# Attention and two feed-forward layers on one core: the first layer's rounding moved from VectorE to ScalarE, a third tile for decoded weights, and a new order of issue

## The chip, the cores and the metric

The kernel runs on one core of a Trainium2 chip, in one launch. The metric is the device time of that core in microseconds, the median of three runs. The engines are named as the profile names them: PE (TensorE, matrix multiply) with PEld (its weight loads), DVE (VectorE), ACT (ScalarE), POOL (GpSimd) and SP (SyncE, which here only issues DMAs). Each engine takes its own instructions strictly in the order in which they were written, so an instruction that waits holds up all that stand behind it on that engine.

## The reference

Three stages, one behind the other, in float32:

```python
# 1: attention, q, k, v of (4, 8, 576, 64): 32 heads
scores = scale * q @ k.T
thresh = max(scores, axis=-1) - tau
scores = where(scores >= thresh, scores, -1e9)
attn = exp(scores - max(scores)); attn = attn / (sum(attn) + 1e-9)
x = (attn @ v) as (2304, 512)
# 2: first feed-forward layer, w_in (512, 2048), w_out (2048, 512)
h = x @ w_in
x = (h * cos(h)) @ w_out
# 3: second feed-forward layer, its own weights
r = maximum(x @ w_in, 0)
out = (s * r * r + b) @ w_out
```

## The kernel before

**Attention.** The 32 heads are worked as 16 pairs of two heads, a pair as 9 tiles of 128 queries against 576 keys. One tile's chain is: PE forms the scores `s` (L318, L325) into one of two PSUM buffers; DVE reduces them to the row minimum `mn` (L332; keys are negated, so it stands for the maximum); POOL adds tau to it (`thr`, L336); ACT takes the exponential `e` (L340); DVE compares, multiplies and sums in one instruction (`p`, L346), which gives the score buffer back. PE turns finished tiles (`pt`, L281, and the rest of the tiles as `ptr`, L378), ACT stores them (L296, L300), and PE multiplies them with the values (`av`, L430), for the pair before, between the score tiles of the running pair. DVE's reciprocal of the row sums (`r<-sm`, L399) is issued once per pair.

**Weights.** They lie in DRAM as 64-bit words, 32 half blocks per layer: for each of 16 slices `f` of the hidden dimension, part 0 (input weights) and part 1 (output weights). `decode` (L179) makes two float tiles, `wh` and `wl`, from one half block: a DMA into a raw tile `wr` (two of them, L534), the magnitude on ACT (L538), a clamp on POOL (L542), three integer instructions on DVE, called shift, sign and fill here (L545, L550, L555), the high part `wh` (on POOL for the first 15 half blocks, L564, later on ACT, L568), and the low part `wl` on POOL (L189). Between the magnitude and `wl` the words lie in a tile `wt`, of which there are two. The first 15 half blocks of layer 1 (`EARLY`) have room in memory while attention runs; the other 17 get theirs when attention has ended. A half block's name in the rows is `wt_f_part`.

**Feed-forward layers.** Each layer runs over five blocks of tokens (four of 512, one of 256) and in each over the 16 slices, 72 steps of 512 columns per layer. One step has 12 hidden matmuls (`h`, L657, into one of four PSUM banks), the stages of the activation, and 12 output matmuls (`acc`, L758 in the first layer, L760 in the second). Products are formed three times, from high and low parts, so every operand is split in two. At a block's start its tokens are split into `x` tiles: ACT writes the high part (L631), DVE subtracts (L634, shown as L189) for each of 4 column groups. The stages of a first-layer step (L692 to L737) are: the rounding to integers `s0` on DVE, from the bank (L694, which the profile shows as helper line L687), the remainder `s1` on DVE (L697), a clamp on POOL (L700), the sine on ACT with the bias tile `hpi` (L705, helper line L226), the product with `h` on DVE (L708), which frees the bank, the high part `gh` on ACT, and the low part `gl` on POOL (L189). Stages of a step are called by these names below.

**The order.** Nothing is issued as it is written in the source. `Order` (L28) holds every piece of work with its engine, a length in nanoseconds that is written by hand (`add(engine, length, rank, ...)`), a rank and what it must wait for. `run` (L80) then plays the engines forward: each engine takes, of the first `WINDOW` pieces by rank, the first one that can begin within `SLACK` ns of the earliest, and the resulting order is the one that is issued. Ranks come from the tables `PAIR` and `PLACE` (L119 to L126): `early` and `early_step` set the rank, in pairs, of the 15 early half blocks; `first`, `second` and their steps that of the later ones. A tile whose buffers are all in use can't be drawn, so the sizes in `ring` (L219) shape the order as well.

Of the kernel before, what the change touches and what calls it, by code (L numbers as in the profile page):

```python
# [10 lines left out]
F32 = mybir.dt.float32  # L11
# [6 lines left out]
P = 128  # L18
# [9 lines left out]
class Order:  # L28
# [3 lines left out]

    SLACK = 262
    LAG = 90
    WINDOW = 48

# [77 lines left out]
EARLY = 15  # L116

WEIGH = (3, 4)
PAIR = 16840  # L119

PLACE = {
    "scores": -6086, "stat": -3181, "exp": -7313, "mask": 1993, "turn": 1108, "turned": 3152, "rest": 443,
    "rested": -1757, "sums": 1929, "weigh0": -252, "weigh1": 4687, "weigh_step": 1086, "finish": -4708,
    "normalise": 40063, "keys": -30127, "early": 3.337, "early_step": 1.142, "first": 3.121, "second": 1.354,
    "second_step": 0.963, "first_step": 0.523, "xin": -10749, "active": 5021, "output": 5748,
}  # L126
STEP = 5450

# [2 lines left out]
def attention_moe_moe2_kernel(  # L131
# [37 lines left out]
    nc.scalar.dma_start(out=tau_t, in_=tau)  # L169
    hpi = cpool.tile([P, 1], F32, name="hpi")  # L170
    nc.vector.memset(hpi, math.pi / 2)

    warm = cpool.tile([P, 1], F32, name="warm")
    nc.scalar.activation(warm, hpi, AF.Exp)
# [23 lines left out]

    for half in halves[:EARLY]:
        open_w(half)  # L200
    wtp = ctx.enter_context(tc.tile_pool(name="wtp", bufs=2))
    mg = ctx.enter_context(tc.tile_pool(name="mg", bufs=2))


# [13 lines left out]

    for name, size in (  # L219
        ("s", 2), ("pt", 4), ("q", 2), ("k", 1), ("ks", 2), ("v", 2), ("e", 2), ("p", 12), ("PT", 2),  # L220
        ("rb", 1), ("xs", 1), ("wr", 2), ("wt", 2), ("r", 2), ("gh", 2), ("gl", 2), ("mn", 6), ("thr", 6),
    ):
        ring(name, size)

# [8 lines left out]
    def pair(n):  # L233
# [70 lines left out]
        for i in range(9):  # L304
# [37 lines left out]
            def mask(i=i):  # L342
                if "sm" not in T:
# [4 lines left out]
                    accum_out=T["sm"][:, i : i + 1],  # L348
                )

            s_ = add("PE", 600 if i == mixed else 500, at + PLACE["scores"], scores, after=[lq, ks] if i == 0 else [], take=[ts],
                     give=[tk["q"], tk["ks"]] if i == 8 else [], tail=250)
            scored.append(s_)
            m_ = add("DVE", 755, at + PLACE["stat"], stat, after=[s_], take=[tm])
            t_ = add("POOL", 190, at + PLACE["stat"], limit, after=[m_], take=[th])
# [3 lines left out]
            if i in (1, 3, 4, 6, 8):  # L359
                tiles = [i] if i == mixed else [i - 1, i]  # L360
                tt = [ticket("pt"), ticket("pt")]
                r_ = add("PE", 280 * len(tiles), at + PLACE["turn"], lambda t=tiles: turn(t), after=[masks[j] for j in tiles],
                         take=[*tt, *([tk["PT"]] if i == 1 else [])], tail=170)
                for g in (1, 0):
                    c_ = add("ACT", 170 + 215 * len(tiles), at + PLACE["turned"], lambda g=g, t=tiles: store_turned(g, t),
                             after=[r_], give=[tt[g]])
                    transposed.append(c_)
# [152 lines left out]
    def decode(half, rank, opened):  # L520
# [53 lines left out]
        o = add("SP", 60, rank - 6000, load, take=[tr], tail=4000)  # L574
        o = add("ACT", 675, rank, magnitude, after=[o], take=[tt])
        o = add("POOL", 620 if early else 720, rank, clamp, after=[o])
        o = add("DVE", 430 if early else 600, rank, shift, after=[o])
        o = add("DVE", 690 if early else 1030, rank, sign, after=[o])
        o = add("DVE", 690 if early else 1150, rank, fill, after=[o], give=[tr])
        o = add("POOL" if early else "ACT", 630, rank, high, after=[o, opened], take=[tw])  # L580
        o = add("POOL", 1270 if early else 1370, rank, low, after=[o], give=[tt])
# [34 lines left out]
    def blocks_of(layer, blk):  # L616
# [25 lines left out]
        def step(fs):  # L642
# [43 lines left out]
            def mult_add(o, x, s1, s2_):  # L686
                nc.vector.tensor_scalar(out=o, in0=x, scalar1=s1, scalar2=s2_, op0=ALU.mult, op1=ALU.add)  # L687

            e = w / 0.96
            if layer == 0:  # L690

                def s0():  # L692
                    tiles()
                    mult_add(B["r"].bitcast(I32), B["h"], 1.0 / TWO_PI, 0.25)  # L694

                def s1():
                    nc.vector.scalar_tensor_tensor(B["r"], B["r"].bitcast(I32), -TWO_PI, B["h"], ALU.mult, ALU.add)  # L697

                def s2_():
                    nc.gpsimd.tensor_scalar(  # L700
                        out=B["r"], in0=B["r"], scalar1=RMAX, scalar2=RMIN, op0=ALU.min, op1=ALU.max
                    )

                def s3():
                    act(B["r"], B["r"], AF.Sin, bias=hpi)  # L705

                def s4():
                    nc.vector.tensor_tensor(B["r"], B["h"], B["r"], ALU.mult)  # L708

                def s5():  # L710
                    tiles_g()
                    act(B["gh"], B["r"], AF.Copy)

                stages = [
                    ("DVE", 150 + e, s0, [rt], []), ("DVE", 150 + e, s1, [], []), ("POOL", 790, s2_, [], []),
                    ("ACT", 720, s3, [], []), ("DVE", 150 + e, s4, [], [ht]), ("ACT", 630, s5, [ght], []),
                ]
            else:
                def s0():
                    tiles()  # L720
                    act(B["r"], B["h"], AF.Relu)

                def s1():
                    act(B["r"], B["r"], AF.Square)

                def s2_():
                    mult_add(B["r"], B["r"], s_t, b_t)

                def s3():
                    tiles_g()  # L730
                    nc.vector.tensor_copy(B["gh"], B["r"])  # L731

                stages = [
                    ("ACT", 600, s0, [rt], [ht]), ("ACT", 630, s1, [], []), ("DVE", 550, s2_, [], []),
                    ("DVE", 430, s3, [ght], []),
                ]
# [147 lines left out]
```

## Time and profile before

| | us |
|---|---|
| median of 3 runs (1146.82 to 1151.14) | 1147.77 |
| the profiled execution | 1150.11 |
| its span, first to last instruction | 1148.3 |
| PE busy | 1075.1 (94%) |
| DVE busy | 657.6 (57%) |
| ACT busy | 483.7 (42%) |
| POOL busy | 455.2 (40%) |
| mean granted clock of TensorE, share of full speed | 0.98 |

The span falls into attention (0 to about 313 us; the last pair's reciprocal is issued at 313.25), the first layer (its first hidden matmul at 313.80, blocks to about 830) and the second layer (to the end). Weights of the first layer are decoded during attention and in the layer's first block; those of the second layer from about 660 to 830 us. The page's busy time of PE is not PE at its peak: what a stretch of PE is worth is read from the number of its matmuls in it.

### The profile page before, as it was taken

Reading aid. Unit: us, or ns where it says so; the run is one execution under the profiler, and the core shown is the slowest. Engines: PE = TensorE matmul, PEld = TensorE weight load, DVE = VectorE, ACT = ScalarE, POOL = GpSimd, SP = SyncE. Lnnn points to the kernel's source line nnn. Section 1 sums busy time; section 2 is a strip of 40 time slices with the busy share of each in tenths; the row PEclk is TensorE's granted clock in tenths of the full one; section 3 lists DMA queues with packets and bytes.
Section 4 is the critical chain, followed back from the end, with each engine's and each line's share of the span. In section 5 each row is a group of like instructions: output and inputs, shape, how many; then the busy total and the mean of one; then the engine's idle time right before and its main releaser. Section 6 shows DMA issues by size and latency. Waiting matters only on the chain.

```text
span 1148.3 us, 17581 instructions
## 1 busy us (share of the span) xinstructions
PE 1075.1 (94%) x6736; PEld 816.2 (71%) x6736; DVE 657.6 (57%) x1062; ACT 483.7 (42%) x880; POOL 455.2 (40%) x556
## 2 busy tenths in 40 slices
PE   5988897889799889999999999999999999999998
PEld 3544444444467657889988877788888898888886
DVE  5778888788888864344553677887821222112211
ACT  4767776667644342222322343454422222223221
POOL 1133424233377744333333466676632222222222
PEclk9989999999899989999999999999999999999999
DMA  4232423232132211000010012333200000000100
GB/s 163 65 115 79 137 83 133 83 115 73 60 103 92 91 57 36 1 1 1 1 37 1 19 58 87 95 91 93 74 37 1 1 37 1 19 1 1 37 1 37
DMA packets 23507, 63.59 MB, mean 55 GB/s; under 512 B 4464, under 2 KB 4736, under 8 KB 23424
## 3 DMA queue, kind: packets, MB, share of 16 engines
q1 hardware_dynamic: 23280, 62.48, 16.8%
q8 instruction: 53, 0.87, 0.3%
q14 instruction: 30, 0.25, 0.1%
q10 hardware_dynamic: 144, 0.00, 0.0%
HBM read 57.67 MB, written 4.79 MB: 54 GB/s over the span
## 4 chain that ended last, share of the span: by engine, by line
PE 70%; DVE 14%; issue 7%; POOL 5%; ACT 2%; DMA 1%; POOLq 0%; DVEq 0%; ACTq 0%; SPq 0%
PE h L657 27%; PE acc L760 14%; PE acc L758 12%; PE s L318 7%; PE av L430 6%; DVE wt L550 3%; PE pt L281 2%; DVE p L346 2%; DVE wt L555 2%; DVE wt L545 2%; DVE mn L332 2%; DVE r L687 1%; POOL r L700 1%; PE s L325 1%; POOL wt L542 1%
## 5 line engine op out<-in xcount | busy, mean ns | idle before, releaser
L657 PE MATMUL h<-x,wh 128*128 128x512 f32 (+1 forms) x1280 | 371.2, 375 | 8.3 <-DVE r L708 6.3
L189 POOL TENSOR_TENSOR gl<-r,gh 128x512 fp32r<-128x512 f32 x144 | 190.8, 1325 | 306.5 <-DVE gh L731 242.1
L657 PEld LDWEIGHTS h<-x,wh 128*128 128x128 f32 x1280 | 232.3, 189 | 59.4 <-DVE r L708 9.4
L657 PE MATMUL h<-x,wl 128*128 128x512 f32 (+1 forms) x640 | 239.4, 374 | 0.3 <-POOL wl L189 0.3
L687 DVE TENSOR_SCALAR r<-r,s_t,b_t 128x512 f32<-128x512 f32 x72 | 44.0, 613 | 191.5 <-ACT r L226 191.5
L318 PE MATMUL s<-ks,q 64*128 64x288 f32 x512 | 108.4, 500 | 47.4 <-DVE p L346 35.0
L226 ACT ACTIVATE r<-h 128x512 f32<-128x512 f32 x72 | 43.2, 599 | 232.8 <-PE h L657 215.9
L657 PEld LDWEIGHTS h<-x,wl 128*128 128x128 f32 x640 | 120.8, 189 | 23.9 <-POOL wl L189 0.9
L332 DVE TENSOR_REDUCE mn<-s 128x1 f32<-128x576 f32 x144 | 108.9, 756 | 46.0 <-PE s L318 39.7
L340 ACT ACTIVATE e<-s,mn 128x576 f32<-128x576 f32 x144 | 106.5, 739 | 51.2 <-DVE mn L332 49.1
L346 DVE SCALAR_TENSOR_TENSOR p<-s,thr,e 128x576 f32<-128x576 f32 x144 | 116.2, 814 | 14.4 <-ACT e L340 10.0
L758 PE MATMUL acc<-gh,wh 128*128 128x512 f32 (+1 forms) x320 | 119.1, 372 | 4.0 <-ACT wh L568 4.0
L758 PE MATMUL acc<-gl,wh 128*128 128x512 f32 (+1 forms) x320 | 119.2, 372 | 2.6 <-POOL gl L189 2.6
L226 ACT ACTIVATE r<-r,hpi 128x512 f32<-128x512 f32 x72 | 51.9, 721 | 163.8 <-POOL r L700 163.6
L758 PE MATMUL acc<-gh,wl 128*128 128x512 f32 (+1 forms) x320 | 119.2, 372 | 0.1
L760 PE MATMUL acc<-wh,gl 128*128 128x512 f32 x288 | 112.6, 391 | 0.0
L760 PE MATMUL acc<-wl,gh 128*128 128x512 f32 x288 | 112.4, 390 | 0.0
L760 PE MATMUL acc<-wh,gh 128*128 128x512 f32 x288 | 112.3, 390 | 0.0
L318 PEld LDWEIGHTS s<-ks,q 64*128 64x128 f32 x512 | 45.8, 208 | 86.2 <-issue 52.4
L189 POOL TENSOR_TENSOR wl<-wt,wh 128x512 fp32r<-128x512 f32 x64 | 89.9, 1405 | 39.5 <-ACT wh L568 38.8
L336 POOL TENSOR_TENSOR thr<-mn,ptau 128x1 f32<-128x1 f32 x144 | 32.4, 227 | 176.5 <-DVE mn L332 170.8
L430 PE MATMUL av<-PT,v 128*64 128x288 f32 x640 | 96.2, 420 | 0.0
(64 smaller groups left out, 1436.5 us busy)
## 6 DMA issues: line engine op xcount, KB each, us to landing
wr<-in_w_dram SPq DMA_DIRECT2D x64, 512.0 KB, 3.6
q<-in_qt_dram SPq DMA_DIRECT2D x15, 576.0 KB, 3.8
v<-in_va_dram SPq DMA_DIRECT2D x16, 320.0 KB, 3.6
k<-in_kt_dram SPq DMA_DIRECT2D x16, 288.0 KB
out_dram<-ob SPq DMA_DIRECT2D x18, 256.0 KB, 2.2
rb<-rd SPq DMA_DIRECT2D x16, 144.0 KB, 3.4
rb<-rd SPq DMA_DIRECT2D x16, 128.0 KB, 3.1
q<-in_qt_dram SPq DMA_DIRECT2D x1, 448.0 KB
```

The source lines that it names most:

```text
L189: (eng or nc.gpsimd).tensor_tensor(out=o, in0=a, in1=b.bitcast(F32), op=ALU.subtract)
L226: nc.scalar.activation(o, x, fn, **kw)
L318: nc.tensor.matmul(st[:, h, :H2], T["q"][g, c : c + 128], T["ks"][g, hd * H2 : (hd + 1) * H2], start=True, stop=True,)
L332: nc.vector.tensor_reduce(out=T["mn", i], in_=T["s", i][:, :, :H2], axis=mybir.AxisListType.XY, op=ALU.min)
L340: nc.scalar.activation(T["e", i], T["s", i][:, :, :H2], AF.Exp, bias=T["mn", i], scale=-1.0)
L346: nc.vector.scalar_tensor_tensor(out=p, in0=T["s", i][:, :, :H2], scalar=T["thr", i], in1=T["e", i], op0=ALU.is_le, op1=ALU.mult, accum_ou ...
L430: nc.tensor.matmul(T["av", h][g, :H2], T["v"][:, hd, k, :], T["PT"][:, 4 if k == 4 else k + 5 * hd, h * H2 : (h + 1) * H2], start=(k == 0) ...
L550: nc.vector.scalar_tensor_tensor(out=T["t"], in0=T["raw"][:, :, 1], scalar=0x3FFFFFFF, in1=T["t"], op0=ALU.bitwise_or, op1=ALU.bitwise_and)
L657: nc.tensor.matmul(B["h"][:, e * n : (e + 1) * n], wt[:, c * P : (c + 1) * P], x, start=(c == 0 and j == 0), stop=(c == HP - 1 and j == 2),)
L687: nc.vector.tensor_scalar(out=o, in0=x, scalar1=s1, scalar2=s2_, op0=ALU.mult, op1=ALU.add)
L758: nc.tensor.matmul(acc[d][:, :n], wt[:, d * P : (d + 1) * P], g, **st)
L760: nc.tensor.matmul(acc[d], g[:, d * P : (d + 1) * P], wt, **st)
```

## The change

Three edits, and the tables that set the order are drawn anew.

- The first layer's rounding `s0` becomes an ACT instruction: identity with scale 1/(2 pi) and a bias tile `quarter` of 0.25, which reads the bank and writes integers. DVE has 72 instructions fewer, ACT 72 more.
- There are three `wt` tiles in place of two (the pool and the ring of the order).
- `SLACK`, `PAIR`, 17 of the entries of `PLACE` and several lengths are other numbers.

```diff
-    SLACK = 262
+    SLACK = 202
...
-PAIR = 16840
+PAIR = 15080
...
-    "normalise": 40063, "keys": -30127, "early": 3.337, "early_step": 1.142, "first": 3.121, "second": 1.354,
-    "second_step": 0.963, "first_step": 0.523, "xin": -10749, "active": 5021, "output": 5748,
+    "normalise": 40063, "keys": -25720, "early": 1.893, "early_step": 0.845, "first": 3.121, "second": 0.648,
+    "second_step": 1.057, "first_step": 0.523, "xin": -5835, "active": 8769, "output": 5748,
...
+    quarter = cpool.tile([P, 1], F32, name="quarter")
+    nc.vector.memset(quarter, 0.25)
...
-    wtp = ctx.enter_context(tc.tile_pool(name="wtp", bufs=2))
+    wtp = ctx.enter_context(tc.tile_pool(name="wtp", bufs=3))
...
-        ("rb", 1), ("xs", 1), ("wr", 2), ("wt", 2), ("r", 2), ("gh", 2), ("gl", 2), ("mn", 6), ("thr", 6),
+        ("rb", 1), ("xs", 1), ("wr", 2), ("wt", 3), ("r", 2), ("gh", 2), ("gl", 2), ("mn", 6), ("thr", 6),
...
-            s_ = add("PE", 600 if i == mixed else 500, at + PLACE["scores"], scores, after=[lq, ks] if i == 0 else [], take=[ts],
-                     give=[tk["q"], tk["ks"]] if i == 8 else [], tail=250)
+            s_ = add("PE", 660 if i == mixed else 620, at + PLACE["scores"], scores, after=[lq, ks] if i == 0 else [], take=[ts],
+                     give=[tk["q"], tk["ks"]] if i == 8 else [], tail=130)
...
-        o = add("DVE", 430 if early else 600, rank, shift, after=[o])
-        o = add("DVE", 690 if early else 1030, rank, sign, after=[o])
+        o = add("DVE", 430 if early else 900, rank, shift, after=[o])
+        o = add("DVE", 690 if early else 1100, rank, sign, after=[o])
...
-                    mult_add(B["r"].bitcast(I32), B["h"], 1.0 / TWO_PI, 0.25)
+                    act(B["r"].bitcast(I32), B["h"], AF.Identity, scale=1.0 / TWO_PI, bias=quarter)
...
-                    ("DVE", 150 + e, s0, [rt], []), ("DVE", 150 + e, s1, [], []), ("POOL", 790, s2_, [], []),
+                    ("ACT", 600, s0, [rt], []), ("DVE", 150 + e, s1, [], []), ("POOL", 790, s2_, [], []),
```

In the changed kernel's rows every line number stands 2 higher. Three places of the order are shown. The first is DVE at the end of attention, before: `p_8` is the last pair's last tile, the four `x` rows split the first block's tokens.

```order
L346 SCALAR_TENSOR_TENSOR p_7_4471,sm_4232<-s_7_4430,thr_7_4464,e_7_4466 128x576
L189 TENSOR_TENSOR x_4460<-xT,x_4460 128x512
L189 TENSOR_TENSOR x_4461<-xT,x_4461 128x512
L189 TENSOR_TENSOR x_4462<-xT,x_4462 128x512
L189 TENSOR_TENSOR x_4463<-xT,x_4463 128x512
L346 SCALAR_TENSOR_TENSOR p_8_4508,sm_4232<-s_8_4445,thr_8_4469,e_8_4498 128x576
L545 TENSOR_SCALAR wt_5_1_4239<-wt_5_1_4239 128x512
L399 RECIPROCAL r_4533<-sm_4232 128x9
L550 SCALAR_TENSOR_TENSOR wt_5_1_4239<-wr_5_1_4180,wt_5_1_4239 128x512
L555 SCALAR_TENSOR_TENSOR wt_5_1_4239<-wr_5_1_4180,wt_5_1_4239 128x512
L545 TENSOR_SCALAR wt_7_0_4506<-wt_7_0_4506 128x512
```

The same place of DVE now, from the last pair's last two tiles on:

```order
L348 SCALAR_TENSOR_TENSOR p_7_4501,sm_4279<-s_7_4458,thr_7_4479,e_7_4481 128x576
L348 SCALAR_TENSOR_TENSOR p_8_4509,sm_4279<-s_8_4462,thr_8_4497,e_8_4499 128x576
L401 RECIPROCAL r_4537<-sm_4279 128x9
L191 TENSOR_TENSOR x_4473<-xT,x_4473 128x512
L191 TENSOR_TENSOR x_4474<-xT,x_4474 128x512
L191 TENSOR_TENSOR x_4475<-xT,x_4475 128x512
L191 TENSOR_TENSOR x_4476<-xT,x_4476 128x512
L547 TENSOR_SCALAR wt_8_0_4598<-wt_8_0_4598 128x512
L699 SCALAR_TENSOR_TENSOR r_0_0_4614<-r_0_0_4614,h_4516 128x512
L552 SCALAR_TENSOR_TENSOR wt_8_0_4598<-wr_8_0_3497,wt_8_0_4598 128x512
```

The tokens' split has moved behind the last tile, and the next half block is 8_0: before, the early half blocks 5_1, 7_0 and 6_1 stood here too; now all 15 early ones are decoded among the tiles of attention.

The second place is DVE in the first layer's first block, before: `r_0_6` and `r_0_7` are the tiles of steps 6 and 7.

```order
L555 SCALAR_TENSOR_TENSOR wt_10_0_4883<-wr_10_0_4845,wt_10_0_4883 128x512
L545 TENSOR_SCALAR wt_9_1_4930<-wt_9_1_4930 128x512
L708 TENSOR_TENSOR r_0_6_4925<-h_4530,r_0_6_4925 128x512
L687 TENSOR_SCALAR r_0_7_4970<-h_4531 128x512
L697 SCALAR_TENSOR_TENSOR r_0_7_4970<-r_0_7_4970,h_4531 128x512
L550 SCALAR_TENSOR_TENSOR wt_9_1_4930<-wr_9_1_4899,wt_9_1_4930 128x512
L555 SCALAR_TENSOR_TENSOR wt_9_1_4930<-wr_9_1_4899,wt_9_1_4930 128x512
L708 TENSOR_TENSOR r_0_7_4970<-h_4531,r_0_7_4970 128x512
```

And now, at the same half blocks:

```order
L557 SCALAR_TENSOR_TENSOR wt_10_0_4850<-wr_10_0_4812,wt_10_0_4850 128x512
L547 TENSOR_SCALAR wt_9_1_4898<-wt_9_1_4898 128x512
L710 TENSOR_TENSOR r_0_5_4893<-h_4517,r_0_5_4893 128x512
L552 SCALAR_TENSOR_TENSOR wt_9_1_4898<-wr_9_1_4860,wt_9_1_4898 128x512
L699 SCALAR_TENSOR_TENSOR r_0_6_4939<-r_0_6_4939,h_4516 128x512
L557 SCALAR_TENSOR_TENSOR wt_9_1_4898<-wr_9_1_4860,wt_9_1_4898 128x512
L710 TENSOR_TENSOR r_0_6_4939<-h_4516,r_0_6_4939 128x512
```

The rounding is gone from DVE, and half block 9_1 stands one step earlier beside the steps (5 and 6 in place of 6 and 7).

The third place is POOL in that block, before:

```order
L700 TENSOR_SCALAR r_0_8_5017<-r_0_8_5017 128x512
L542 TENSOR_SCALAR wt_10_1_5022<-wt_10_1_5022 128x512
L189 TENSOR_TENSOR gl_0_7_5036<-r_0_7_4970,gh_0_7_5027 128x512
L189 TENSOR_TENSOR wl_11_0_5043<-wt_11_0_4975,wh_11_0_5042 128x512
L700 TENSOR_SCALAR r_0_9_5062<-r_0_9_5062 128x512
L542 TENSOR_SCALAR wt_12_0_5067<-wt_12_0_5067 128x512
```

And now, where the half blocks 10_1 and 12_0 are clamped:

```order
L544 TENSOR_SCALAR wt_10_1_4988<-wt_10_1_4988 128x512
L702 TENSOR_SCALAR r_0_7_4985<-r_0_7_4985 128x512
L191 TENSOR_TENSOR gl_0_6_5007<-r_0_6_4939,gh_0_6_5000 128x512
L191 TENSOR_TENSOR wl_11_0_4994<-wt_11_0_4944,wh_11_0_4993 128x512
L544 TENSOR_SCALAR wt_12_0_5034<-wt_12_0_5034 128x512
L702 TENSOR_SCALAR r_0_8_5031<-r_0_8_5031 128x512
```

From half block 10_1 on the clamp of the next words stands ahead of the step's clamp; before, it always stood behind it.

On PE the largest change is in attention: groups of 8 value matmuls ahead of one score tile stood 15 times in the 16 pairs, and stand 6 times now. Between the first layer's first and sixteenth output groups stood 14 output groups and 16.75 hidden groups (of 12 matmuls); now 14 and 16.

## Rows read from the trace of the kernel before

**Rows 1.** PE's matmul groups in a full stretch (start us, us, what).
```profile
602.31 2.73 PE acc L758 x12
605.05 2.79 PE h L657 x12
```

**Rows 2.** Stretches: busy us (x instructions) of PE, PEld, DVE, ACT, POOL; granted clock, DMA.
```profile
400.00:425.00 25.00, 20.48 (x73) 14.96 (x72) 18.04 (x24) 10.05 (x16) 12.00 (x14) 0.86 0.26 84
675.00:750.00 75.00, 71.89 (x308) 56.93 (x307) 60.27 (x75) 32.77 (x53) 48.37 (x47) 1.00 0.28 85
```

**Rows 3.** DVE and PE at attention's end: start us, us, engine line, what, idle before.
```profile
308.78 3.29 DVE L189 TENSOR_TENSOR x<-xT,x 128x512 fp32r<-128x512 f32 x4
...
312.00 0.80 DVE L346 SCALAR_TENSOR_TENSOR p<-s,thr,e 128x576 f32<-128x576 f32 x1
...
313.80 1.22 PE L657 MATMUL h<-x,wh 128*128 128x512 f32 x2
...
318.86 0.69 PE L378 MATMUL ptr<-ident,p 64*64 64x64 f32 x32
...
321.07 3.13 PE L430 MATMUL av<-PT,v 128*64 128x288 f32 x24
...
325.73 2.16 PE L430 MATMUL av<-PT,v 128*64 128x288 f32 x16
...
334.66 0.39 PE L758 MATMUL acc<-gh,wh 128*128 128x512 f32 x1
```

**Rows 4.** First shift of 8_0, last fill and low part of 15_1; PE's sixteenth output.
```profile
327.98 0.42 DVE L545 TENSOR_SCALAR wt<-wt 128x512 int32<-128x512 int32 x1
...
435.03 0.98 DVE L555 SCALAR_TENSOR_TENSOR wt<-wr,wt 128x512 int32<-128x512 int32 x1
...
436.83 1.30 POOL L189 TENSOR_TENSOR wl<-wt,wh 128x512 fp32r<-128x512 f32 x1 [1.36 <-ACT wh L568]
...
438.53 2.73 PE acc L758 x12
```

**Rows 5.** DVE and POOL in the first layer's first block, two half blocks.
```profile
381.57 1.50 DVE L545 TENSOR_SCALAR wt<-wt 128x512 int32<-128x512 int32 x1 [1.21 <-POOL wt L542]
...
383.59 0.67 DVE L687 TENSOR_SCALAR r<-h 128x512 int32<-128x512 f32 x1
...
390.62 0.68 DVE L687 TENSOR_SCALAR r<-h 128x512 int32<-128x512 f32 x1
...
392.18 0.91 POOL L700 TENSOR_SCALAR r<-r 128x512 f32<-128x512 f32 x1 [2.03 <-DVE r L697]
393.17 0.61 POOL L542 TENSOR_SCALAR wt<-wt 128x512 f32<-128x512 f32 x1
...
393.82 1.48 DVE L545 TENSOR_SCALAR wt<-wt 128x512 int32<-128x512 int32 x1 [1.20 <-POOL wt L542]
```

**Rows 6.** Groups by line: busy us, mean ns, idle before and its releasers.
```profile
L687 DVE TENSOR_SCALAR r<-h 128x512 int32<-128x512 f32 x72 | 49.5, 687 | 71.2 <-PE h L657 63.4 <-POOL gl L189 4.9 <-POOL r L700 2.6
L226 ACT ACTIVATE r<-r,hpi 128x512 f32<-128x512 f32 x72 | 51.9, 721 | 163.8 <-POOL r L700 163.6
```

**Rows 7.** Waits: engine line, waited for; us in total, times, longest.
```profile
DVE mn L332 <- PE s L318: 39.7, 64, 2.2
ACT wt L538 <- POOL wl L189: 18.3, 11, 2.4
```

**Rows 8.** DVE in attention: all 16 reciprocals, then rows of the timeline.
```profile
L399 DVE RECIPROCAL r<-sm x16: 203/205/216, 29.1 to 313.3; 128x9 f32<-128x9 f32 x16
...
48.10 0.21 DVE L399 RECIPROCAL r<-sm 128x9 f32<-128x9 f32 x1
...
75.71 0.76 DVE L332 TENSOR_REDUCE mn<-s 128x1 f32<-128x576 f32 x1 [1.13 <-PE s L318]
...
158.64 1.62 DVE L332 TENSOR_REDUCE mn<-s 128x1 f32<-128x576 f32 x2
...
162.11 1.61 DVE L332 TENSOR_REDUCE mn<-s 128x1 f32<-128x576 f32 x2
```

More of the change, by code (lines that the diff above doesn't have):

```diff
@@ L118 @@
 WEIGH = (3, 4)
-PAIR = 16840
+PAIR = 15080
 PLACE = {
-    "scores": -6086, "stat": -3181, "exp": -7313, "mask": 1993, "turn": 1108, "turned": 3152, "rest": 443,
-    "rested": -1757, "sums": 1929, "weigh0": -252, "weigh1": 4687, "weigh_step": 1086, "finish": -4708,
-    "normalise": 40063, "keys": -30127, "early": 3.337, "early_step": 1.142, "first": 3.121, "second": 1.354,
-    "second_step": 0.963, "first_step": 0.523, "xin": -10749, "active": 5021, "output": 5748,
+    "scores": -7792, "stat": -3181, "exp": -7313, "mask": 1319, "turn": 942, "turned": 2047, "rest": 302,
+    "rested": -1757, "sums": 882, "weigh0": 136, "weigh1": 4789, "weigh_step": 1171, "finish": -1970,
+    "normalise": 40063, "keys": -25720, "early": 1.893, "early_step": 0.845, "first": 3.121, "second": 0.648,
+    "second_step": 1.057, "first_step": 0.523, "xin": -5835, "active": 8769, "output": 5748,
 }
@@ L361, in pair @@
                 tt = [ticket("pt"), ticket("pt")]
-                r_ = add("PE", 280 * len(tiles), at + PLACE["turn"], lambda t=tiles: turn(t), after=[masks[j] for j in tiles],
+                r_ = add("PE", 310 * len(tiles), at + PLACE["turn"], lambda t=tiles: turn(t), after=[masks[j] for j in tiles],
                          take=[*tt, *([tk["PT"]] if i == 1 else [])], tail=170)
```

## The prediction, made before the changed kernel ran

> **What bounds the kernel now.** I read the busy shares by stretch first, then the chain that ended last, then the timelines of DVE, POOL and PE at the places where the chain leaves PE. From the second block on PE is the bound: one step is an output group of 2.73 us and a hidden group of 2.79 us, 5.52 us in all [rows 1], and they stand end to end. Such a stretch has 110 matmuls in 25 us; from 400 to 425 there are 73, and the granted clock fell to 0.86, so part of it ran at 1.2 GHz behind PE's own idle time; from 675 to 750 there are 308 where 75 / 5.52 x 24 = 326 fit [rows 2]. So PE is short of work in two places, the first layer's first block and the last one before the second layer, and both are places where weights are decoded. The third place is attention, where PE waits for DVE and DVE for PE, and the fourth is the seam between attention and the first layer. I take the four in turn, from one fixed point: m, the end of the last pair's eighth tile on DVE, 308.78 here, where the token splits begin [rows 3].
>
> **The seam.** Before, the four splits of the tokens (3.29 us) stand ahead of the ninth tile, so the last transposes, and behind them the first hidden matmul, come late: it starts at 313.80, m + 5.0, the hidden group ends at 318.86, m + 10.1, and the first output group starts at 334.66, m + 25.9 [rows 3]. In the new order the ninth tile comes first (0.8 us), the reciprocal takes 0.2, and each split of 0.82 us releases 0.7 us of hidden matmuls: the first hidden group ends at m + 0.8 + 0.2 + 3.3 + 0.7 = m + 5.0. Then PE has the rest of the turning (0.69), the rows of sums (0.2), 40 records of value matmuls (3.1 + 2.1 = 5.2 by the two rows of 24 and 16) and three hidden groups (8.4), 14.5 us [rows 1, 3]. First output: m + 19.6 at the earliest, 6.3 us sooner.
>
> **The first block.** What ends it is the last half block, 15_1. Before, 17 decodes run from 327.98 (m + 19.2) to the last fill's end at 436.0: 108.0 / 17 = 6.36 us each. Its low part is ready 2.1 us later, at 438.13, and the sixteenth output group is that of 438.5, m + 129.7 [rows 4]. PE had done 0.75 hidden group more by then than it will have in the new order, so the like-for-like point is m + 127.6. In the new order the first of the same 17 decodes can start at m + 4.3, since the three early half blocks that stood here are done, and there are two limits:
> - PE: from the first output on, 15 output and 16 hidden groups, 15 x 2.73 + 16 x 2.79 = 85.6, so m + 105.2.
> - Decoding: m + 4.3 + 17 p + 2.3, p the pace. With p unchanged, 6.36: m + 114.7. With all of the rounding (0.67 and 0.68 us in two decodes [rows 5]) off the path, p = 5.68: m + 103.2, which is under PE's limit.
>
> Is the rounding on the path? The two shifts at 381.57 and 393.82 lie 12.25 us apart, that is two decodes and two steps, more than PE's 11.04. The shift waits for POOL's clamp of the words, that one stands behind POOL's clamp of the step, and this waited 2.03 us for DVE's remainder, which stands behind the rounding [rows 5]. So it is on the path before. But DVE and POOL also take turns: the shift that takes 0.42 us at 327.98 takes 1.50 at 381.57, beside POOL's long subtractions [rows 4, 5]. When the rounding goes, some of the time that it used is then spent in such turns. The third wt tile, and the words' clamp ahead of the step's from 10_1 on, loosen the loop. I take half of the rounding's time as won, p near 6.0, and m + 109. Gain for the seam and the block: 127.6 - 109 = 18.6 us, bounds 12.9 (pace unchanged) and 22.4 (PE's limit).
>
> **What ACT takes on.** The 72 roundings cost DVE 687 ns each, 49.5 us; on ACT the nearest row is the sine, also with a bias tile, 721 ns [rows 6]. In the slow stretch ACT was busy 10.05 of 25 us [rows 2]; 4.5 steps x 0.72 = 3.2 us more leave it half idle, so the work itself is hidden, and what it can cost is only its place in the queue (a rival below). The order has the same two table loads on ACT as before.
>
> The rows give the rounding nearly one price on either engine. The Trainium skill, in ScalarE: Activation LUTs, section Rules for kernel authors, speaks against the edit: additions and multiplications belong on VectorE, which it puts at up to about three times ScalarE's rate in bf16. By that rule the step would pay some 1.4 us more on ACT (an estimate from that page), seen at the five block starts of the layer, where nothing covers the first step's chain: 7 us, and 1130. The trace does not bear it out for these float32 operands from PSUM (687 against 721 ns), so it gets no share of the sum.
>
> **The stretch from 675 to 750.** 326 - 308 = 18 matmuls at 0.23 us, 4.1 us [rows 1, 2], lost in the same loop of decode and step. Bounds 0 and 4.1; I take 3, since 16 decodes that start earlier are spread over more steps and need a smaller gain in pace than the first block.
>
> **Attention.** Three more half blocks are decoded in it: 9 DVE instructions of 0.4 to 0.8 us, about 6 us, their POOL and ACT work and three 512 KB loads, which move up on SP's queue between the loads of q, k and v. What hides them? A pair in which nothing is decoded takes 48.10 - 29.1 = 19.0 us; the mean of 15 pairs, with 36 such instructions in 16 pairs, is (313.3 - 29.1) / 15 = 18.95 [rows 8]. So they fit into DVE's waits for scores, of which there are 39.7 us in 64 pieces [rows 7]. The largest are like that of 75.71, 1.13 us, where eight value matmuls stood ahead of the score tile [rows 8]. Groups of eight stand 15 times before and 6 times now; 9 x 0.6 (the mean wait, 39.7 / 64) = 5.4 us could go, less what the finer splitting brings anew. Bounds: a loss of 6 (nothing hidden any more), and on the other side DVE without any wait: two tiles in 162.11 - 158.64 = 3.47 us [rows 8], so 15 pairs x 4.5 x 3.47 = 234 plus 15 decodes of about 2 us = 264, against 284.2 between the first and the last reciprocal: a gain of 20. I stay near the measured indifference and take a gain of 3.5.
>
> **Sum.** 3.5 + 18.6 + 3 = 25 us. The profiled execution took 1150.11 (span 1148.3), so 1125 for one like it; the median of the runs shown, 1147.77, lies 2.3 us lower, so the forecast is 1123. Nothing behind 830 us changes: PE is full there.
>
> **Rivals.**
> 1. One of the two uncertain terms fails: the three decodes are not hidden (attention loses 6, no gain of 3.5: 1132), or the pace stays at 6.36 because POOL sets it, and the later stretch gains nothing (25 - 5.7 - 3 = 16: 1131). For it: the turns of DVE and POOL. Against: decoding starts 15 us earlier by the order alone. 1132.
> 2. Both fail: 12.9 - 6 = 7 us, 1141. For it speaks only that both engines' loops are tight.
> 3. Attention gains 13, two thirds of its bound, with score tiles in smaller gaps: 1113. For it: the waits above. Against: the moved decodes use the same gaps.
> 4. Slower: the rounding queues on ACT behind work that waits. ACT is strictly in order, and magnitudes waited for POOL's low parts 11 times, 1.7 us in the mean [rows 7]. If every decode put that much between the bank and the remainder, p = 8.1 and the block ends at m + 144, 16 us later than m + 127.6; with attention's 3.5 that is 1160. It decides from p = 7.1 on, 0.75 us more per decode than before. Against: the third wt tile lets the magnitude go ahead of that low part.
>
> **How the numbers follow.** Forecast 0.52, rival 1 0.24, rival 2 0.06, rival 3 0.11, rival 4 0.07. A measurement of this kernel tells about 0.5% (5.7 us) from no change, so faster means under 1142: the forecast, rivals 1 and 3, and half of rival 2, with a little off for terms I misjudge together, 0.88; within it 0.06; slower 0.06. The range reaches from under rival 3 to the near side of rival 2: 1110 to 1139. The forecast's own range, by the block's bounds, is 1119 to 1129.
>
> **What would show it.** In the changed profile: the first output group 19 to 22 us behind the eighth tile of the last pair; the first 15 decodes before the last reciprocal; a pace of 5.7 to 6.2 us from 8_0 to 15_1; no half clock around 410; some 320 matmuls in the 75 us before the second layer; the last reciprocal near 310. Wrong would be a last reciprocal beyond 316, a pace over 6.4, or ACT's rounding waiting behind a high part while its hidden group is done.

## The result, and the profile after

The changed kernel takes 1132.8 us, the median of four runs (1132.11 to 1138.02). The kernel before, run beside it, took 1149.45 (1146.82 to 1153.2); the ratio is 0.9863, 95% interval 0.982 to 0.9905. So it is faster by 17 us, where 25 were forecast. The profiled execution took 1132.11, its span is 1130.3.

Five points of the two traces show where the 18.0 us between the spans come from. For the sixteenth output, the first block's last, the point of before is the like-for-like one of the prediction, m + 127.6.

| point (us) | before | after | won up to here | won on this leg |
|---|---|---|---|---|
| m, eighth tile of the last pair done on DVE | 308.78 | 304.15 | 4.6 | 4.6 |
| first output group | m + 25.9 | m + 21.1 | 9.4 | 4.8 |
| sixteenth output group | m + 127.6 | m + 113.5 | 18.7 | 9.3 |
| first output group of the second layer | 757.37 | 735.93 | 21.4 | 2.7 |
| end of the span | 1148.3 | 1130.3 | 18.0 | -3.4 |

The fourth point is read from the timelines of PE, before and after:

```profile
757.37 0.39 PE L760 MATMUL acc<-wh,gh 128*128 128x512 f32 x1
735.93 0.40 PE L762 MATMUL acc<-wh,gh 128*128 128x512 f32 x1
```

The rows of after that answer to [rows 3, 4], from the timelines of DVE, ACT, POOL and PE (start us, us, engine line, what, idle before it and its releaser), in order of time:

```profile
304.15 0.81 DVE L348 SCALAR_TENSOR_TENSOR p<-s,thr,e 128x576 f32<-128x576 f32 x1
...
305.30 0.21 DVE L401 RECIPROCAL r<-sm 128x9 f32<-128x9 f32 x1 [0.33 <-POOL sm L397]
305.58 3.53 DVE L191 TENSOR_TENSOR x<-xT,x 128x512 fp32r<-128x512 f32 x4
...
305.72 0.49 PE L659 MATMUL h<-x,wh 128*128 128x512 f32 x1
307.36 0.50 PE L659 MATMUL h<-x,wh 128*128 128x512 f32 x1 [1.14 <-DVE x L191]
...
308.91 0.69 ACT L540 ACTIVATE wt<-wr 128x512 f32<-128x512 f32 x1
...
310.12 0.69 PE L380 MATMUL ptr<-ident,p 64*64 64x64 f32 x32
...
310.34 0.43 DVE L547 TENSOR_SCALAR wt<-wt 128x512 int32<-128x512 int32 x1 [1.23 <-POOL wt L544]
...
325.25 0.39 PE L760 MATMUL acc<-gh,wh 128*128 128x512 f32 x1
...
409.62 0.69 DVE L557 SCALAR_TENSOR_TENSOR wt<-wr,wt 128x512 int32<-128x512 int32 x1
...
411.50 0.69 ACT L228 ACTIVATE r<-h,quarter 128x512 int32<-128x512 f32 x1 [1.23 <-POOL gl L191]
412.48 0.63 ACT L228 ACTIVATE gh<-r 128x512 fp32r<-128x512 f32 x1 [0.29 <-DVE r L710]
...
413.01 0.61 ACT L570 ACTIVATE wh<-wt 128x512 fp32r<-128x512 f32 x1
...
413.19 1.30 POOL L191 TENSOR_TENSOR gl<-r,gh 128x512 fp32r<-128x512 f32 x1 [1.72 <-ACT gh L228]
...
415.26 1.29 POOL L191 TENSOR_TENSOR wl<-wt,wh 128x512 fp32r<-128x512 f32 x1
```

The splits follow the ninth tile, and hidden matmuls start at 305.72 where they started at 313.80. At the block's end the last half block's fill is done at 410.31, but its high part starts on ACT only at 413.01: ahead of it in ACT's queue stand a rounding, which waited 1.23 us for POOL's `gl`, and a `gh`. On POOL the low part then stands behind another `gl`. So 6.2 us lie between fill and finished low part, at 416.55, where [rows 4] had 2.1. The sixteenth output group starts 1.1 us later still, at 417.67: it stands on PE behind 21 hidden matmuls, which run without a pause from 412.50 and had waited for the product of an earlier step on DVE, the instruction that frees the bank (the chain below).

Stretches of after, against [rows 2] (columns as there): the half clock around 410 is gone, 99 matmuls in place of 73, and 315 in place of 308.

```profile
400.00:425.00 25.00, 23.52 (x99) 17.98 (x98) 12.68 (x20) 12.46 (x20) 11.16 (x12) 1.00 0.14 42
675.00:750.00 75.00, 73.29 (x315) 58.75 (x314) 52.87 (x68) 39.51 (x66) 48.37 (x45) 1.00 0.27 80
```

The chain that ended last, of after (start us, us, what): first a piece of the first block, then one of a full stretch, against [rows 1].

```profile
387.53 1.52 DVE wt L547
...
389.08 1.69 DVE wt L552
...
390.78 0.99 DVE wt L557
...
391.83 3.58 DMA wr<-in_w_dram
...
395.49 0.67 ACT wt L540
...
397.41 1.54 DVE wt L547
...
398.97 1.69 DVE wt L552
...
400.68 0.69 DVE wt L557
...
411.75 0.70 DVE r L710
...
412.50 5.17 PE h L659 x21
417.67 2.75 PE acc L760 x12
...
608.44 2.81 PE h L659 x12
611.25 2.76 PE acc L760 x12
```

Two things here were not forecast. The full step of PE is 2.81 + 2.76 = 5.57 us, not 5.52, at the same granted clock of 1.00: a loss wherever PE is full. And in the first block the chain runs from a fill through the DMA that fills the raw tile it freed: with two raw tiles `wr` a tile comes back only after DMA, magnitude, clamp, shift, sign and fill.

Waits of after (total us, times, longest), against [rows 6, 7]: DVE waits 10 us less for scores, and the rounding on ACT now waits for `gl`, which gives back the `r` tile of two steps earlier. The 18.7 us of the second line hold two instructions of that helper line: 15.5 are the rounding's, as the group below shows (DVE's rounding had 4.9 [rows 6]), and 3.1 belong to the second layer.

```profile
DVE mn L334 <- PE s L320: 29.7, 56, 2.2
...
ACT r L228 <- POOL gl L191: 18.7, 21, 2.7
...
ACT wt L540 <- DMA wr<-in_w_dram: 14.2, 12, 3.4
```
```profile
L228 ACT ACTIVATE r<-h,quarter 128x512 int32<-128x512 f32 x72 | 49.4, 685 | 94.5 <-PE h L659 78.8 <-POOL gl L191 15.5
```

### The profile page after: what moved, and what is told of

Its sections match the earlier page's. It is cut to its first block, busy times and chain, and to the rows that moved or that the text cites. A ratio compares the mean times of both kernels' runs of the same rounds, so it can differ in the third digit from the quotient of the medians.

```text
span 1130.3 us, 17459 instructions
## 1 busy us (share of the span) xinstructions
PE 1067.5 (94%) x6736; PEld 809.8 (72%) x6736; DVE 588.5 (52%) x991; ACT 531.0 (47%) x952; POOL 458.3 (41%) x556
## 4 chain that ended last, share of the span: by engine, by line
PE 82%; DVE 7%; POOL 4%; issue 3%; ACT 2%; DMA 1%; SPq 0%; DVEq 0%; ACTq 0%; POOLq 0%
PE h L659 33%; PE acc L762 18%; PE acc L760 14%; PE av L432 7%; PE s L320 6%; PE pt L283 2%; DVE p L348 2%; DVE mn L334 2%; PE s L327 1%; POOL wl L191 1%; ACT e L342 1%; DMA wr<-in_w_dram 1%; POOL r L702 1%; DVE wt L552 1%; POOL gl L191 1%
## 5 line engine op out<-in xcount | busy, mean ns | idle before, releaser
L689 DVE TENSOR_SCALAR r<-r,s_t,b_t 128x512 f32<-128x512 f32 x72 | 40.2, 559 | 214.3 <-ACT r L228 214.3
L320 PE MATMUL s<-ks,q 64*128 64x288 f32 x512 | 100.1, 477 | 46.6 <-DVE p L348 39.7
L762 PE MATMUL acc<-wl,gh 128*128 128x512 f32 x288 | 112.1, 389 | 0.0
L699 DVE SCALAR_TENSOR_TENSOR r<-r,h 128x512 f32<-128x512 int32 x72 | 49.3, 685 | 109.1 <-ACT r L228 106.9
L191 POOL TENSOR_TENSOR wl<-wt,wh 128x512 fp32r<-128x512 f32 x64 | 88.0, 1376 | 28.8 <-ACT wh L570 25.9
L432 PE MATMUL av<-PT,v 128*64 128x288 f32 x640 | 98.6, 429 | 0.0
L338 POOL TENSOR_TENSOR thr<-mn,ptau 128x1 f32<-128x1 f32 x144 | 34.9, 245 | 151.0 <-DVE mn L334 147.6
```

The costliest lines, as they stand in the source:

```text
L191: (eng or nc.gpsimd).tensor_tensor(out=o, in0=a, in1=b.bitcast(F32), op=ALU.subtract)
L320: nc.tensor.matmul(st[:, h, :H2], T["q"][g, c : c + 128], T["ks"][g, hd * H2 : (hd + 1) * H2], start=True, stop=True,)
L432: nc.tensor.matmul(T["av", h][g, :H2], T["v"][:, hd, k, :], T["PT"][:, 4 if k == 4 else k + 5 * hd, h * H2 : (h + 1) * H2], start=(k == 0) ...
L762: nc.tensor.matmul(acc[d], g[:, d * P : (d + 1) * P], wt, **st)
```

## Experiments: each part alone and each part undone

With and without the three parts there are eight kernels. "Old" and "new" order stand for the two tables; the order itself is drawn anew from its table for every kernel, so a row is its parts together with the order that was drawn for them. "Shift" marks those that also hold the new bias tile, of which more below. The last column is the distance from the first to the seventeenth late fill in the profiled execution, over 16: what one late decode takes.

| order | rounding | `wt` tiles | us, median | ratio to before, 95% interval | late decode, us |
|---|---|---|---|---|---|
| old | DVE | 2 | 1149.3 | 1 | 6.60 |
| old | ACT (shift) | 2 | 1149.9 | 1.0005 (0.9987 to 1.0023) | 6.32 |
| old | DVE | 3 | 1150.0 | 1.0017 (0.9998 to 1.0036) | 6.65 |
| old | ACT (shift) | 3 | 1148.8 | 0.9999 (0.9985 to 1.0014) | 6.39 |
| new | DVE | 2 | 1140.6 | 0.9926 (0.9902 to 0.995) | 6.84 |
| new | DVE (shift) | 3 | 1140.5 | 0.9925 (0.9902 to 0.9948) | 6.80 |
| new | ACT (shift) | 2 | 1149.2 | 0.9992 (0.9975 to 1.0008) | 6.81 |
| new | ACT (shift) | 3 | 1132.8 | 0.9863 (0.982 to 0.9905) | 5.97 |

Rows with and without the shift are not quite alike, since the shift itself costs 3 to 5 us, as the next section shows. At an equal place in memory (against b_pad32, ratio 1.0035) the rounding alone on the old order is worth about 3 us (the two intervals just overlap) and the two parts together about 4; "no gain" below is the sum of that and the shift. The last column needs no such correction (the kernel before once more has 6.57, with the shift alone 6.63, the changed kernel without the shift 5.97): on the new order each part alone leaves it where it was, and both together take 0.8 to 0.9 us off.

**b0_again**, the kernel before once more, no edit.

> The kernel before, unchanged, profiled again beside the three kernels below, to learn whether TensorE's step of the late stretches belongs to the kernel or to the run. In the kernel before a step of twelve h and twelve acc matmuls took 2.79 + 2.73 = 5.52 us; in the changed one 2.81 + 2.76 = 5.57 us at the same granted clock of 1.00, which over some 140 steps is 6 to 7 us. Theory 'kernel' (where the tiles lie in SBUF, or what the other engines do, sets the step): 5.52 again here, span about 1148. Theory 'run' (chips or sessions differ by 1%): another step than 5.52, and all four kernels of this call show the same one.

1147.21 us, span 1145.4, step 2.79 + 2.73 again. The step belongs to the kernel, not to the run.

**b_act_only**: the rounding moved, with its bias tile and its place among the stages, nothing else.

```diff
...
-                    mult_add(B["r"].bitcast(I32), B["h"], 1.0 / TWO_PI, 0.25)
+                    act(B["r"].bitcast(I32), B["h"], AF.Identity, scale=1.0 / TWO_PI, bias=quarter)
...
```

> The kernel before with the first layer's rounding alone moved to ScalarE (old table of places, two decoded-word tiles). Theory DVE (VectorE bounds the first block, so 17 times 0.69 us comes off it): pace of the fills in the first block 6.36 -> about 5.8, whole kernel 8 to 12 us less, ratio 0.990 to 0.993. Rival 'ring' (the two decoded-word tiles and the chain through them bound the block): pace unchanged within 0.1, kernel within 3 us. Rival 'ACT queue' (ScalarE's in-order queue holds the rounding behind work that is not ready): slower by 3 to 10 us. If the 4 bytes by which the new bias tile moves the later tiles set TensorE's step, the late steps read 5.57 instead of 5.52 us here and in no other kernel of this call but those with that shift.

No gain, so theory DVE as it was put falls for the whole kernel. In the trace the block's last fill starts at 429.44, where before it was 435.03, and the second layer's first output at 755.48 (757.37): some 2 us are won there, and the later layer, with its longer step, gives them back. A late decode takes 0.28 us less, not the whole 0.69 of the rounding.

**b_wt3_only**: `wt` pool and ring 3 in place of 2.

> The kernel before with a third tile for decoded words and nothing else. Theory DVE: VectorE still carries the same work in the first block, so at most 3 us less, ratio 0.997 to 1.000. Rival 'ring': the wait of the magnitude for a tile (18.3 us over the run) goes, and with it 8 to 18 us, ratio 0.984 to 0.993. If 2 KB of shift of the later tiles set TensorE's step, late steps read 5.57 us here.

No gain; the rival falls. The step was 5.52, as it should be: the tile's 2 KB move later tiles by a multiple of 64 bytes.

**b_tab_only**: `SLACK`, `PAIR`, `PLACE` and lengths of the changed kernel; rounding and tiles as before.

> The kernel before with the new table of places, pair period, slack and measured lengths alone (rounding on VectorE, two decoded-word tiles). Theory 'sum of parts': the 4.6 us of attention and about 5 us of the seam are the table's, the first block keeps its pace of 6.2 to 6.4: 7 to 11 us less, ratio 0.990 to 0.994. Rival 'only together': the table was drawn for three tiles and a free VectorE; with two tiles decoding starts late or stalls, and the kernel gains 4 us at most or loses. Its tiles lie where those of the kernel before lie: by the theory of addresses the late step is 5.52 us.

8.7 us less, as the sum of parts said. The eighth tile of the last pair is done at 301.21 (308.78 before), and the first output stands at 321.66, 13.0 us sooner. The first late fill comes 20.7 us sooner (308.80 for 329.45), but then a decode takes 6.84 us, so the block itself wins nothing: at its sixteenth output, with as many hidden groups done, some 12 us are left, at the second layer's first output 10.5 (746.84 for 757.37).

**a_round_dve**: the changed kernel with the rounding on DVE.

> The changed kernel with the rounding put back on VectorE (its place in the order drawn anew by the same rules); the small bias tile stays where it is, so the later tiles do not move. Moving the rounding alone gave nothing on the old table (1149.9 us against 1149.3), the new table alone gave 8.7 us. Theory 'interaction' (with the new table VectorE is the slow member of the first block, so the rounding counts there): pace of the fills back from 5.9 to 6.2 to 6.4, 1138 to 1143 us, as the table alone. Rival 'third tile' (the decoded-word tile is what the table needs): 1131 to 1135 us.

1140.5: the interaction. The last fill starts at 419.57, 10 us later than in the changed kernel. The time is as expected, the pace is not: 6.80 us a decode, where 6.2 to 6.4 was expected, from a first late fill that comes 3.2 us sooner (310.81 for 314.05).

**a_two_wt**: the changed kernel with two `wt` tiles.

> The changed kernel with two tiles for decoded words again. Theory 'third tile counts once VectorE is free': the magnitude waits for a tile again, the first block is 4 to 8 us longer, 1136 to 1141 us. Rival 'raw tiles' (the two raw-word tiles, freed by the fill and filled by a DMA of 3.6 us, bound the decodes either way): within 2 us of the changed kernel, 1131 to 1135 us.

1149.2: not 4 to 8 but 16 us lost, with the rounding on ACT the whole gain. Timelines of DVE and ACT of this kernel, the late decodes' first magnitudes and the second and third fill:

```profile
310.38 0.68 ACT L540 ACTIVATE wt<-wr 128x512 f32<-128x512 f32 x1
313.85 0.67 ACT L540 ACTIVATE wt<-wr 128x512 f32<-128x512 f32 x1
...
320.14 0.68 DVE L557 SCALAR_TENSOR_TENSOR wt<-wr,wt 128x512 int32<-128x512 int32 x1
...
324.55 1.14 ACT L570 ACTIVATE wh<-wt 128x512 fp32r<-128x512 f32 x2
...
327.96 0.66 ACT L540 ACTIVATE wt<-wr 128x512 f32<-128x512 f32 x1
...
335.94 1.80 DVE L557 SCALAR_TENSOR_TENSOR wt<-wr,wt 128x512 int32<-128x512 int32 x1
```

The late half blocks have room for their high parts only when attention has ended. Until then two decodes are done and hold both tiles, so the third magnitude stands behind the first low part (POOL, 326.22 to 327.51) and runs at 327.96; with three tiles it ran at 320.71, and the third fill at 326.83 instead of 335.94. From the third fill to the last, 14 decodes take 6.31 us each here and 5.91 in the changed kernel, so part of the pace hangs on the third tile too. The block is not all of it: from 675 to 750 us there are 296 matmuls (315 in the changed kernel), some 4 us. This kernel is slower even than the new order alone (1140.6), which has the same pace. In the two profiled executions 4.1 of the 8.5 us between them stand there already at m (305.35 for 301.21) and 3.5 come behind the second layer's first output, where the shift counts. Whether the 4.1 in attention belong to the kernel or to the execution isn't settled by these runs.

**b_act_wt3**: the last corner, both parts on the old order.

> The kernel before with the rounding on ScalarE (and its bias tile, so the 32-byte shift) and the third tile for decoded words, but with the old table of places, period, slack and lengths: the last corner of the eight with and without each part. Either part alone gave nothing on the old table; on the new one they gave nothing singly and 8 us together (1140.6 to 1132.8, in spite of the shift's 3 to 5 us). Theory 'the two together free the first block, whatever the table': the table's own 8.7 us are missing, 1139 to 1143 us. Rival 'the table has to place the decodes for it' (the old lengths of 600 and 1030 ns for shift and sign and the old places of the x splits keep the late decodes behind): 1146 to 1151 us.

1148.8: the rival. The last reciprocal is at 312.14 and the last fill at 428.97, so neither attention nor the block's end has moved to where the new table puts them. Still the second layer's first output comes 5.7 us sooner than before (751.63); 4.3 of them are lost behind it, where the shift counts.

## Experiments: TensorE's longer step

The bias tile `quarter` holds 4 bytes a partition, takes 32 in the layout, and stands ahead of nearly everything. In the memory layouts of the two programs the weights' first tile starts at byte 46432 before (32 modulo 64) and 46464 after (0 modulo 64), and the tiles of `gh` and `gl` move in the same way, while the `x` tiles, laid from the other side, stay at 32 modulo 64.

**a_no_shift**: the constant is written into the tile of the warm-up, so nothing moves.

```diff
-    quarter = cpool.tile([P, 1], F32, name="quarter")
-    nc.vector.memset(quarter, 0.25)
...
     nc.scalar.activation(warm, hpi, AF.Exp)
+    quarter = warm
+    nc.vector.memset(quarter, 0.25)
```

> The changed kernel with the bias constant 0.25 kept in the tile that the warm-up writes, so that no new tile is placed ahead of the weights and every later tile lies 32 bytes lower, as in the kernel before. Theory 'address' (b_act_only and the changed kernel, both with the tile, show acc matmuls of 394 and 393 ns in the last layer, all kernels without it 391 and 390): steps of 5.52 instead of 5.57 us, the last layer from first to last output 386 instead of 390 us, the kernel 4 to 7 us less, 1126 to 1129 us. Rival 'ScalarE' (its reading of the bank, not the address, slows TensorE): 5.57 us again, 1131 to 1134 us.

1127.57 us, ratio 0.9818 (0.9797 to 0.9839), 5.2 us under the changed kernel. From the second layer's first output to the end it takes 391.5 us, where the changed kernel takes 394.4 and the kernel before 390.9. The fourteen profiled executions fall into the same two groups: the seven with the shift take 392.9 to 395.8 us for it, the seven without (a_pad64 among them) 390.8 to 392.3.

**b_pad32**: the kernel before with an unused tile in that place.

```diff
+    spare = cpool.tile([P, 1], F32, name="spare")
+    nc.vector.memset(spare, 0.25)
```

> The kernel before with one unused 4-byte tile, placed where the changed kernel has its bias tile, so that all later tiles lie 32 bytes higher; its instructions are otherwise the same. Theory 'address': steps of 5.57 instead of 5.52 us and 4 to 7 us more, 1153 to 1157 us, ratio 1.003 to 1.006. Rival 'not the address alone': within 2 us, 1147 to 1152 us.

1153.05 us, ratio 1.0035 (1.0017 to 1.0054), 3.1 us more than the kernel before beside it, a little under the 4 to 7 expected; of its instructions only one memset is new, and the order is the same on every engine. So the place is shown as the cause, at 3.1 us from this side and 5.2 from the other.

**a_pad64**: the changed kernel with that unused tile as a second one, 64 bytes in all.

> The changed kernel with a second unused 4-byte tile behind the bias tile: later tiles lie 64 bytes higher than in the kernel before, 32 higher than in the changed one. Theory 'where in 64 bytes' (the weights start at 32 modulo 64 in the kernel before, at 0 in the changed one, and the x tiles at 32 in both): steps of 5.52 us again, 1126 to 1129 us. Rival 'any shift from the place of before costs': 5.57 us, 1131 to 1135 us.

1126.73 us, ratio 0.9797 (0.9768 to 0.9826). The chains of a_no_shift, b_pad32 and a_pad64 in a full stretch, in this order:

```profile
607.67 2.79 PE h L659 x12
610.46 2.73 PE acc L760 x12
```
```profile
603.35 2.81 PE h L659 x12
606.16 2.76 PE acc L760 x12
```
```profile
607.75 2.76 PE h L661 x12
610.51 2.77 PE acc L762 x12
```

5.52, 5.57 and 5.53 us. A shift by 32 bytes costs 0.05 us a step, 64 bytes don't; but with 64 the parts are others (2.76 and 2.77), so the place modulo 64 bytes is not all there is to it. Which of the operands' places it hangs on was not tried.

## Experiments: what bounds the first block now

**a_third_r**: a third `r` tile, from a pool opened when attention has ended.

```diff
...
-                B["r"] = mg.tile([P, NB], F32, tag="r", name=f"r{nm}")[:, :w]
+                pool = wpools["r"] if i % 3 == 2 else mg
+                B["r"] = pool.tile([P, NB], F32, tag="r", name=f"r{nm}")[:, :w]
...
```

> The changed kernel with a third tile for the activation's r (every third step takes it from a pool opened when attention is over). Theory 'r ring' (the rounding's wait for the low part of two steps earlier, 18.7 us over the run and on the chain of waits from 350 to 385 us, bounds the first block): that wait goes below 5 us, fills at 5.6 to 5.7 us, 3 to 6 us less, 1127 to 1130 us. Rival 'raw tiles' (a fill frees a raw tile, its DMA takes 3.6 us, then magnitude, clamp, shift, sign, fill: some 11.8 us for two decodes): the wait moves, pace stays 5.8 to 5.9, within 1.5 us of the changed kernel.

1133.36 us, the rival. The rounding's wait for `gl` is gone from the list, and the magnitude's wait for the DMA of raw words rose to 18.6 us in 17 waits from 14.2 in 12. The sixteenth output comes at m + 112.1, 1.4 us sooner, with a quarter of a hidden group (0.7 us) less ahead of it; but the stretch before the second layer, in its newly drawn order, has 305 matmuls where the changed kernel has 315:

```profile
675.00:750.00 75.00, 71.62 (x305) 56.52 (x304) 52.40 (x64) 39.06 (x66) 48.09 (x44) 1.00 0.25 78
```

**a_raw3**: a_no_shift with a third tile for raw words, in every third late decode.

```diff
...
-            T["raw"] = small.tile(
+            T["raw"] = (wpools["wx"] if extra else small).tile(
...
```

> The changed kernel without the 32-byte shift (its time 1127.6 us) and with a third tile for raw words, which every third late decode takes from a pool opened when attention is over. A third r tile gave nothing, and the chain of waits from 387 to 402 us runs fill, DMA 3.58, magnitude 0.67, clamp 0.62, shift 1.5, sign 1.7, fill 1.0. Theory 'raw tiles' (a raw tile comes back each 11.8 us, so two of them give a fill each 5.9 us): ScalarE's wait for the DMA of raw words in the first block goes from 6 to below 2 us, fills at 5.6 to 5.7, TensorE's idle time around 381 to 417 us shrinks, 3 to 8 us less, 1120 to 1125 us. Rival 'engines' (clamp, low parts and gl on GpSimd, 5 us a step, and VectorE's 5 us a step beside them bound the block): pace within 0.1, 1126 to 1129 us.

1124.14 us, ratio 0.978 (0.9751 to 0.9809), the fastest of all. The interval overlaps that of a_no_shift, so the 3.4 us between the medians are not clear of the noise, and the pace rests on the trace; in the profiles the second layer's first output stands at 731.07 against 734.10. ACT's wait for the DMA of raw words between 305 and 420 us is 0.6 us, in a_no_shift 6.1. From the fourth to the sixteenth fill a decode takes 4.65 us (338.84 to 394.58), where the changed kernel takes 5.57 (333.84 to 400.68); over all 17, by the prediction's formula, it is 5.65 for 5.88, as the third fill comes late (334.06 for 327.29 in a_no_shift). The sixteenth output is at m + 106.7. One hidden group fewer stands ahead of it than in the changed kernel, so like for like that is m + 109.5, 4.0 us sooner and 4.3 us above PE's limit of m + 105.2. Its stretch and a piece of its chain:

```profile
400.00:425.00 25.00, 24.71 (x107) 19.55 (x106) 10.59 (x17) 11.23 (x18) 10.37 (x11) 1.00 0.07 22
```
```profile
377.31 0.72 POOL r L706
...
378.12 1.62 POOL wl L191
379.74 1.70 POOL gl L191
...
381.53 0.61 POOL wt L548
382.14 1.26 POOL wl L191
```

The DMA is gone from this part of the chain; POOL's own instructions stand nearly end to end.

## Why the prediction was right in kind and 10 us off

| term | forecast | measured |
|---|---|---|
| attention | 3.5 | 4.6 |
| seam and first block | 18.6 | 14.1 |
| stretch before the second layer | 3 | 2.7 (4.7 in a_no_shift) |
| behind it | 0 | -3.4 (-0.6 in a_no_shift) |
| sum | 25 | 18 (22.7 in a_no_shift) |

The two profiled executions' own distance is the sum's; the medians lie 16.7 apart. So 7 of the 10 us between 1123 and 1132.8 are in these terms. The other 3 are in how executions and medians lie: the forecast took off 2.3 because the profiled execution lay above the median, and the changed kernel's lies 0.7 below its own. The time is inside the stated range of 1110 to 1139 and outside the forecast's own, 1119 to 1129.

- **"Nothing behind 830 us changes: PE is full there" failed**: it took the duration of a matmul as fixed. Behind 830 us 3.4 us are lost, and by a_no_shift another 2.0 of the stretch before; all in all the shift by 32 bytes costs 5.2 us by a_no_shift and 3.1 by b_pad32, about as much as the first block misses, 4.5. Why a place in memory changes the duration of a matmul, no run here shows.
- **The first block: m + 113.5, not m + 109.** The formula was m + 4.3 + 17 p + 2.3. The pace was right: (410.31 - 310.34) / 17 = 5.88 for p near 6.0, 2.0 us better in sum. The start was not: the first late shift came at m + 6.2, since its magnitude stands on ACT behind splits and turned tiles. And the end was not: the last low part is done 6.2 us behind its fill, at m + 112.4, with the last high part behind a rounding and a `gh` in ACT's queue, and the output comes 1.1 us later, since PE is then in its 21 hidden matmuls. So "what ends it is the last half block" holds only in part: the chain runs through hidden groups that wait for the step's own stages. Before, too, PE ran without a pause from 432.70 to the output group at 438.53, with the low part ready at 438.13. Rival 4's mechanism shows in the rounding that waits in ACT's queue ahead of the high part, but not by the sign named for it, a rounding behind a high part: what it waits for is `gl`, 15.5 us in the run. The third `r` tile removes those waits and at most 1.4 us of this delay, so they are little of it.
- **Half of the rounding's time as won** named nearly the right size with an incomplete reason. The rounding's move alone takes 0.28 us off a late decode on the old order, and nothing on the new one with two `wt` tiles; with the new order and the third tile it takes off 0.83, more than the rounding's own 0.69. The third tile, which the prediction took as one that loosens the loop, is what the whole gain hangs on once the rounding is on ACT. What the loop closes over then is, by the trace of a_raw3, the two raw tiles, which the prediction didn't consider; a third `r` tile gave nothing.
- **The seam**: m + 21.1 for m + 19.6. The reciprocal waited 0.33 us for POOL's sum, the splits began at m + 1.4 instead of m + 1.0, and the first hidden group ended at 310.1, m + 6.0, not m + 5.0.
- **Attention**: the 15 early decodes are hidden, as the last reciprocal's 305.30 (near 310 forecast) and the shorter waits for scores show. That attention gains is shown by more than this pair: m lies at 306.0 to 309.0 in the six profiled executions with the old order and at 299.5 to 305.4 in the eight with the new one, 4.4 us apart in the mean. The size in one pair of executions should not be read as shown: see the last section.
- **What ACT takes on**: 72 roundings of 685 ns in the mean, under the 721 that the sine gave, and DVE's 687. The Trainium skill's rule in ScalarE: Activation LUTs, section Rules for kernel authors, which puts such arithmetic on VectorE, would have given 1130 by the prediction's estimate; the time is near it, but not for that reason, as the rounding's length is the same on both engines.
- Rival 1 had the time, 1132, by luck and for other reasons: it made attention lose or the pace stay, and neither happened.

## What to carry to other kernels

A stage that is bound by a loop over several buffers and engines gives little for one link alone: on the new order the rounding's move or the third tile alone left a late decode at 6.8 us, and both together took it to 6.0. The next link (here the raw tiles) is found by asking on which buffer the new chain closes. Room for decoded work counts most where the consumer can't start yet. And a new constant, however small, moves every tile laid behind it: put it where it moves nothing, and compare the duration of untouched instructions in the two traces before looking for causes elsewhere.

## What the runs showed of the hardware that was not expected

- The place of its operands in SBUF changes TensorE's step: a shift of 32 bytes made 24 matmuls of 128x512 in float32 take 5.57 us for 5.52, at a granted clock of 1.00, and with it the kernel 3 to 5 us longer.
- The same attention code takes different time from execution to execution. In two profiled executions of the kernel before, the last reciprocal came at 313.25 and at 310.43 (b0_again). In a_pad64 it came at 300.59, in a_no_shift, with the same order on other addresses, at 305.77. The granted clock from 100 to 200 us was 1.00 in the one and 0.97 in the other, so stretches at 1.2 GHz can be part of it; how much, and whether the addresses count, is not shown. Single runs of a_pad64 lie up to 9 us apart (1122.1 to 1131.2).
- DVE's shift takes 0.43 us at 310.34 and 1.52 at 387.53, where a 1.30 us subtraction of POOL had begun at 387.46; [rows 4, 5] had the same two lengths, 0.42 and 1.50. The Trainium skill, in SBUF — State Buffer, section Who interferes with whom, says that the loser of the shared pair blocks for the other's whole instruction, and the trace agrees in size: 1.09 us more beside 1.30.
